# A delta-rule attention and two MoE layers on one core: chunk 1 in half steps, its solve placed first, the merge of one chunk a step later, and weight conversions out of VectorE's written order

## The chip, the cores and the metric

The kernel runs on one core of a Trainium2 chip. The metric is the time of one execution in device microseconds, as the median of three runs. All times below are in microseconds unless they are marked ns.

## The reference, cut to what matters

```python
# attention (4 batches, 8 heads, 768 tokens, head size 48), token by token
k_n = k / (norm(k) + 1e-6)
for t in range(S):
    y[t] = q[t] @ state
    state = state + beta[t] * outer(k_n[t], v[t] - k_n[t] @ state)
# x is y as 3072 tokens by 384 features
h = relu(x @ w_in)                 # 384 -> 2048
x = (h * h) @ w_out                # 2048 -> 384
h = max(x @ w1, x @ w2, x @ w3)    # 384 -> 768, three times
out = h @ w_out2                   # 768 -> 384
```

Everything is float32.

## The kernel before

**The chunks.** The 768 tokens are cut into 12 chunks of 64. Within a chunk the recurrence is a triangular system. Its inverse is computed on VectorE for two chunks at a time: one *solve* covers chunks 0 and 1, the next chunks 2 and 3, and so on. A solve (`solve32`, `solve`) works on M, a tile of 128 rows by 32x32 in the memory `buf`. It has a preparation (`prep`: the norms, ten small instructions, then L239), 30 pairs of a multiply (L285) and an add (L287), and a scaling by a (L288). `finish32` then stores the result to DRAM (`xt`, L325, on SP's queue), and `load_x` loads it again on GpSimd's queue into `xb` (L343) and `x1` (L351). What a solve needs is made by `kkps`: for each of four parts, key products on TensorE (`pk` and `pq`, L182), a copy of `pk` on ScalarE (L199), a masked copy of `pq` on VectorE (L200), and stores to DRAM. `start32` loads M from those stores (L304). The keys of a part come through SP's queue (L169).

**Attention of one chunk** (`attention(c)`) has the steps `st0` (products `pA` and `pY` with the state; VectorE scales v by the norms, L437, and subtracts `pA`, L450), `zz` (`pZ`, needs `xb`), `ww` (`pW`), `mm_u` (`pU`), `st2` (`pY` and the new state), `st3` (transposes, which give `xh` and `xl`, the two float32r parts of the chunk's tokens).

**The first MoE layer** of chunk c (`moe_a(c)`) runs beside attention of chunk c+1. It has 8 `s1` groups of 18 matmuls (`p`, L572), each followed by relu, square and cast on ScalarE (L576 to L578, which gives `gh`) and a subtraction on VectorE (L579, which gives `gl`), and 8 `s2` groups of 12 matmuls (`px`, L590), two `s1` behind. Two `p` tiles exist, so `s1` number n+2 cannot start before `gl` number n is computed. The second MoE layer (L951, L968) follows after the last chunk.

PSUM has two buffers under the tag `at`. `pk`, `pq`, `pA`, `pZ`, `pW`, `pU` and the transposes take them in turn, and the next user waits until the last has been read.

**What sets the order.** `moe_a` is a generator that yields after each `s1` and each `s2`. `steps` runs it and, at chosen steps, advances the other generators: `attention`, `kkps`, a solve, the weight conversions. A list such as `[3, 7, 11]` names the steps. From chunk 1 on, `pin` chains every instruction of TensorE and of VectorE behind the one before it in the written order, so that the scheduler can't move them. ScalarE, GpSimd and SP are ordered by the scheduler. Every engine works through its own order from front to back.

In chunks 9 to 11 the weights of the second MoE layer are loaded and split (`w3load`, `turn`): each piece takes a ScalarE instruction (L103), three on VectorE (L106, L109, L110), a cast on ScalarE (L111) and a subtraction on VectorE (L114). In the written order the four VectorE instructions of a piece stand together.

Of the kernel before, what the change touches and what calls it, by code (L numbers as in the profile page):

```python
# [32 lines left out]
LAG = 2  # L33
# [6 lines left out]
def delta_moe(ctx, tc, kc, ab, kt, vt, beta, beta32, beta16, kq, w_in, w_out, w1, w2, w3, w_out2, out):  # L40
# [32 lines left out]

    after, abs_after, cast_after, raw_after, x_after, raws = [], [], [], [], [], []
    parted, last_gl, last_gh = [], [None], [None]
    NR, NP = 3, NF - 7

    def raw_tile(shape):
# [21 lines left out]
    def turn(raw, hi, lo, shape, lo_eng):  # L100
        t = conv.tile([128, *shape], I32, name="cvt", tag="cvt")
        h, l = raw[..., 1], raw[..., 0]
        g = act.activation(out=t.bitcast(F32), in_=h.bitcast(F32), func=AF.Abs, scale=REBIAS)  # L103
        for i in abs_after:
            behind(g.ins, i)
        g = vec.tensor_scalar(out=t, in0=t, scalar1=3, scalar2=None, op0=ALU.logical_shift_left)  # L106
        for i in after:
            behind(g.ins, i)
        vec.scalar_tensor_tensor(out=h, in0=h, scalar=-0x80000000, in1=t, op0=ALU.bitwise_and, op1=ALU.bitwise_or)  # L109
        vec.scalar_tensor_tensor(out=l, in0=l, scalar=29, in1=h, op0=ALU.logical_shift_right, op1=ALU.bitwise_or)  # L110
        g = act.copy(hi, l.bitcast(F32))  # L111
        for i in cast_after:
            behind(g.ins, i)
        parted.append(lo_eng.tensor_tensor(out=lo, in0=l.bitcast(F32), in1=hi.bitcast(F32), op=ALU.subtract).ins)  # L114

    def signed(raw, t, ahead):
        h, u = raw[..., 1], raw.bitcast(U16)
# [140 lines left out]
    def pin():  # L258
        todo = []
        for i in reversed(nc.cur_bb.bb.instructions):  # L260
            if i.name == seen[0]:
                break
            todo.append(i)
        for i in reversed(todo):
            seen[0] = i.name
            if i.engine in pinned:
                if pinned[i.engine]:
                    behind(i, pinned[i.engine])
                pinned[i.engine] = i
# [113 lines left out]
    def attention(c):  # L383
# [68 lines left out]
        def mm_u(p):  # L452
            x, r = tiles[c, p][2], tiles[c, p][6]
            pU = ps_at.tile([128, U2, D], F32, name="pU", tag="at")
            n = U2 - (0 if not c else 2 if p else 4)
            if c:
                free = pYs[p] if p else pxs
                over = free[0].rearrange("p (b n) -> p b n", b=1) if p else free[0]
                over = over[:, :, DM:DM + 2 * D].rearrange("p b (u d) -> p b u d", d=D)
            order = [u for i in range(U2) for u in (i, n + i) if (i < n if u == i else u < U2)]  # L460
            for u in order:
                for t in range(2):
                    if u < n:
                        pe.matmul(pU[half(t), u], x[half(t), u], r[half(t), u], start=True, stop=True)  # L464
                    else:
                        o = over[half(1 - t), (u - n) // 2, (u - n) % 2]
                        i = pe.matmul(o, x[half(t), u], r[half(t), u], start=False, stop=True, skip_group_check=True)
                        for j in free[1:]:
                            behind(i.ins, j)
            u_ = fresh("u", p, 7, [128, U2, D])  # L470
            on_vec = p and c != 1
            def put(to, po):
                if on_vec:
                    last_vec[0] = vec.tensor_copy(to, po).ins
                else:
                    last_act[0] = act.copy(to, po).ins  # L476
            put(u_[:, 0:n], pU[:, 0:n])
            if c:
                for m in range(n, U2, 2):
                    for t in range(2):  # L480
                        put(u_[half(t), m:m + 2], over[half(1 - t), (m - n) // 2])
# [75 lines left out]
            yield  # L557


    def moe_a(c, gp):  # L560
        px = ps_x2.tile([128, 2, 512], F32, name="px", tag="px")
        pxs[:] = [px]
        gs = {}

        def s1(fp):
            p1 = ps_s1.tile([128, 2, TB], F32, name="p1", tag="p1")
            for j in range(2):
                f = slice(128 * (2 * fp + j), 128 * (2 * fp + j + 1))
                n = 0
                for k in range(KD):  # L570
                    for w, x in ((win_h, xh), (win_l, xh), (win_h, xl)):
                        pe.matmul(p1[:, j], w[:, k, f], x[c][:, k], start=n == 0 and j == 0, stop=n == 8, skip_group_check=True)  # L572
                        n += 1
            gh = gp.tile([128, 2, TB], F32R, name="gh", tag="gh", bufs=LAG + 1)
            gl = gp.tile([128, 2, TB], F32R, name="gl", tag="gl", bufs=LAG + 1)
            act.activation(out=p1, in_=p1, func=AF.Relu)  # L576
            act.activation(out=p1, in_=p1, func=AF.Square)  # L577
            last_gh[0] = act.copy(gh, p1).ins  # L578
            last_gl[0] = vec.tensor_sub(out=gl, in0=p1, in1=gh.bitcast(F32)).ins  # L579
            gs[fp] = (gh, gl)  # L580

        def s2(fp):
            gh, gl = gs.pop(fp)
            for h in range(2):
                hs = slice(128 * h, 128 * (h + 1))
                for j in range(2):
                    f = 2 * fp + j
                    wh_, wl_ = (wout[f // 4][:, i, f % 4] for i in range(2))
                    for i, (x, w) in enumerate(((gh, wh_), (gh, wl_), (gl, wh_))):
                        g = pe.matmul(px[:, h, 0:DM], x[:, j, hs], w, start=f == 0 and i == 0, stop=f == NF - 1 and i == 2, skip_group_check=True)  # L590
                        if f == 0 and i == 0:
                            pxs.append(g.ins)

        for fp in range(NF // 2):
            s1(fp)
            if fp == 1 and sums:
                store_sums()
            yield
            if fp >= LAG:
                s2(fp - LAG)  # L600
                yield
        for fp in range(NF // 2 - LAG, NF // 2):
            s2(fp)
            if fp < NF // 2 - 1:
                yield
        xs = conv.tile([128, 2, DM], F32, name="xs", tag="raw", bufs=NR)
        for h in range(2):
            i = vec.transpose(out=xs[:, h], in_=px[:, h, 0:DM])
            if last_vec[0]:
                behind(i.ins, last_vec[0])  # L610
        sums.append((c, xs))
        if c == NC - 1:
            store_sums()
        yield
# [8 lines left out]
    def steps(main, *others):  # L623

        due = [0.0] * len(others)
        for n, _ in enumerate(main, 1):
            pin()
            for i, (rate, g, *_) in enumerate(others):
                due[i] += rate.count(n) if isinstance(rate, list) else rate
                while due[i] >= 1.0:  # L630
                    due[i] -= 1.0
                    next(g, None)
                    pin()
        for rate, g, *keep in others:
            for _ in () if keep else g:
                pin()
# [64 lines left out]
    if True:  # L701
# [19 lines left out]
        def solve32(g, load=(nc.sync, nc.sync), store=((nc.sync,) * 2,) * 2, landing=0):  # L721
# [9 lines left out]
            for n, i in enumerate(solve(vec, M, 32, 64 * len(HALVED[g]), a, tmp32)):  # L731
                for j in solve_after:
                    behind(i.ins, j)
                ops.append(i.ins)
                if g and n == (24 if g > 1 else 12):
                    norm(nm)
                yield
            finish32(g, M, store)
# [156 lines left out]
        for c in range(NC):  # L895
# [3 lines left out]
                extra += [(1.0, weights(3, 2)), (11 / 15.0, later(3, attention(1))), (4.0, later(20, part(solve_next, 10)))]  # L899
            elif c == 1:  # L900
                pinned.update({first_matmul.ins.engine: None, last_gl[0].engine: None})
                extra += [(4.0, solve_next), ([3, 7, 11, 12, 13, 14, 15], attention(2)), ([4, 5, 6, 7, 8, 9, 9, 10], kkps(HALVED[2], (at,)))]
                solve_after[:] = last_vec
                prep_after.clear()
            elif c + 1 < NC:
                extra.append(([1, 2, 5, 7, 10, 12, 14] if c % 2 else [1, 2, 4, 6, 8, 11, 13], attention(c + 1)))
            if c == 2:
                kc_after.clear()
                solve_after.clear()
                extra.append(([1, 5] + [6 + n * 10 // 32 for n in range(32)], solve32(2, landing=1)))  # L910
            elif c in ahead_:
                extra.append(([1 + n * 14 // 32 for n in range(32)], ahead_[c]))
            if c > 1 and c in KK:
                extra.append(([3, 4, 4, 5, 6, 7, 8, 9], kkps(HALVED[KK[c]], (at,))))
                ahead_[c + 1] = solve32(KK[c], landing=1)
# [6 lines left out]
            if c == NC - 1:  # L922
# [2 lines left out]
                first = []  # L925
                extra.append((0.6, chain(load_w3s, w3load((2,)))))
                extra.append((0.5, later(2, x2_steps(0, wb, first))))
            steps(moe_a(c, gp), *extra)
        after.clear()
        abs_after.clear()  # L930

# [111 lines left out]
```

## Time and profile before

| | |
|---|---|
| median of 3 runs (lowest, highest) | 968.87 (968.15, 968.98) |
| the profiled execution's own time | 970.42 |
| its span, first to last instruction | 968.3 |
| TensorE busy | 879.9 (91%), 11422 matmuls |
| VectorE busy | 502.0 (52%) |
| ScalarE busy | 390.8 (40%) |
| GpSimd busy | 149.8 (15%) |
| mean granted TensorE clock | 0.949 of full speed |

The profiled execution took 1.55 longer than the median. TensorE is busy nine tenths of the span, so what a chunk takes is read from where TensorE waits. The chunks in the span, by TensorE's first `p` matmul of each: chunk 1 from 139.6, chunk 2 from 207.3, chunk 3 from 260.5, chunk 4 from 309.15, chunk 9 from 536.65, chunk 10 from 581.98, chunk 11 from 626.95; the second layer starts at 664.1.

### The profile page before, as it was taken

The numbers are of one execution on the slowest core, as the hardware profiler recorded it, in microseconds if no ns is written. First come the engines' busy times: TensorE is split into PE (matmuls) and PEld (weight loads), VectorE is DVE, ScalarE is ACT, GpSimd is POOL, SyncE is SP. The second block draws the span as 40 slices with busy tenths as digits, with TensorE's granted clock in tenths as the row PEclk, the third lists the DMA queues.
The fourth block names the chain that finished last, engine by engine and source line by source line (L and its number), as shares of the span: only waits on it lengthen the run. The fifth ranks groups of instructions, "written<-read, shape, count | busy, mean of one in ns | idle before, by whom it ended". The sixth has DMA issues, their size and how long they took to land.

```text
span 968.3 us, 26547 instructions
## 1 busy us (share of the span) xinstructions
PE 879.9 (91%) x11422; PEld 851.5 (88%) x11422; DVE 502.0 (52%) x1118; ACT 390.8 (40%) x809; POOL 149.8 (15%) x245
## 2 busy tenths in 40 slices
PE   4449867899699999999999998999999999999998
PEld 4438766889689999999999998998999999999998
DVE  2987957237635862685277446566623323323221
ACT  1666862344244444453445355574412212222211
POOL 2251110322212132212311330001100000000000
PEclk8558988899799999999999999999999999999999
DMA  8987723742274248425632633143300110000000
GB/s 196 320 226 194 216 63 84 191 121 63 52 200 115 71 119 212 109 71 136 150 94 62 146 108 84 51 123 107 112 28 25 37 38 25 26 25 17 17 17 33
DMA packets 121125, 98.83 MB, mean 102 GB/s; under 512 B 75904, under 2 KB 101296, under 8 KB 121008
## 3 DMA queue, kind: packets, MB, share of 16 engines
q1 hardware_dynamic: 100224, 58.23, 23.6%
q0 software_dynamic: 11712, 32.41, 12.4%
q10 hardware_dynamic: 9072, 6.49, 2.3%
q8 instruction: 90, 1.47, 0.7%
q14 instruction: 27, 0.22, 0.1%
HBM read 72.45 MB, written 24.64 MB: 100 GB/s over the span
## 4 chain that ended last, share of the span: by engine, by line
PE 74%; DVE 13%; ACT 6%; DMA 4%; issue 2%; POOL 1%; SPq 0%; ACTq 0%; DVEq 0%; POOLq 0%
PE p L951 23%; PE p L572 17%; PE px L590 17%; PE po L968 8%; DVE buf L285 3%; DVE buf L287 2%; DMA xb<-xt 2%; DVE gl L579 2%; PE pU L464 1%; PE pY L514 1%; ACT p L576 1%; ACT p L577 1%; ACT gh L578 1%; PE pk L182 1%; PE pZ L412 1%
## 5 line engine op out<-in xcount | busy, mean ns | idle before, releaser
L951 PE MATMUL p<-x_h,w 128*128 128x384 f32 x864 | 220.1, 336 | 0.0
L590 PE MATMUL px<-wout,gh 128*128 128x384 f32 x768 | 205.2, 348 | 3.9 <-ACT u L476 1.9
L572 PE MATMUL p<-xh,win_h 128*128 128x256 f32 x576 | 169.6, 294 | 4.1 <-DVE gl L579 2.6
L572 PE MATMUL p<-xl,win_h 128*128 128x256 f32 x576 | 163.8, 285 | 1.5 <-DVE xl L536 1.5
L572 PE MATMUL p<-xh,win_l 128*128 128x256 f32 x576 | 163.9, 285 | 0.0
L951 PEld LDWEIGHTS p<-x_h,w 128*128 128x128 f32 x864 | 156.3, 188 | 0.0
L579 DVE TENSOR_TENSOR gl<-p,gh 128x512 fp32r<-128x512 f32 x96 | 66.2, 690 | 163.4 <-ACT gh L578 158.9
L951 PE MATMUL p<-x_l,w 128*128 128x384 f32 x432 | 145.2, 336 | 0.0
L590 PEld LDWEIGHTS px<-wout,gh 128*128 128x128 f32 x768 | 138.9, 194 | 5.8 <-ACT u L476 2.3
L590 PE MATMUL px<-wout,gl 128*128 128x384 f32 x384 | 131.7, 343 | 2.1 <-DVE gl L579 2.1
L576 ACT ACTIVATE p<-p 128x512 f32<-128x512 f32 x96 | 55.9, 582 | 189.2 <-PE p L572 189.2
L572 PEld LDWEIGHTS p<-xh,win_h 128*128 128x128 f32 x576 | 111.1, 193 | 7.7 <-DVE gl L579 3.1
L572 PEld LDWEIGHTS p<-xl,win_h 128*128 128x128 f32 x576 | 110.8, 193 | 2.0 <-DVE xl L536 1.9
L572 PEld LDWEIGHTS p<-xh,win_l 128*128 128x128 f32 x576 | 111.3, 193 | 0.0
L957 DVE TENSOR_TENSOR mx<-p,mx 128x384 f32<-128x384 f32 x48 | 26.7, 557 | 123.1 <-PE p L951 123.0
L951 PEld LDWEIGHTS p<-x_l,w 128*128 128x128 f32 x432 | 81.2, 188 | 0.0
L590 PEld LDWEIGHTS px<-wout,gl 128*128 128x128 f32 x384 | 74.2, 193 | 2.4 <-DVE gl L579 2.4
L959 ACT CAST hh<-mx 128x384 fp32r<-128x384 f32 x48 | 24.6, 513 | 120.0 <-DVE mx L958 120.0
L287 DVE TENSOR_TENSOR buf<-buf 128x30 f32<-128x30 f32 (+9 forms) x180 | 60.4, 336 | 6.0
L285 DVE TENSOR_TENSOR buf<-buf 128x30 f32<-128x30 f32 (+9 forms) x180 | 60.0, 333 | 5.0
L578 ACT CAST gh<-p 128x512 fp32r<-128x512 f32 x96 | 56.4, 587 | 2.5
L577 ACT ACTIVATE p<-p 128x512 f32<-128x512 f32 x96 | 56.0, 583 | 2.5
(183 smaller groups left out, 1347.9 us busy)
## 6 DMA issues: line engine op xcount, KB each, us to landing
kq<-in_kc_dram POOLq DMA_DIRECT2D x22, 448.0 KB, 5.4
raw<-in_moe_w_dram SPq DMA_DIRECT2D x18, 384.0 KB, 3.2
p<-p POOLq DMA_DIRECT2D x22, 256.0 KB, 3.7
raw<-in_moe_w_out_dram SPq DMA_DIRECT2D x13, 384.0 KB, 3.9
v<-in_vt_dram POOLq DMA_DIRECT2D x24, 192.0 KB, 3.2
ktp<-in_kt_dram POOLq DMA_DIRECT2D x24, 192.0 KB, 3.6
x<-xs SPq DMA_DIRECT2D x48, 96.0 KB, 2.8
xr<-x SPq DMA_DIRECT2D x96, 48.0 KB, 1.9
```

The source lines that it names most:

```text
L285: eng.tensor_tensor(out=tv, in0=M[:, 0:j, j].unsqueeze(2).broadcast_to([u, j, m]), in1=M[:, j, j + 1:n].unsqueeze(1).broadcast_to([u, j, m ...
L287: yield eng.tensor_tensor(out=M[:, 0:j, j + 1:n], in0=M[:, 0:j, j + 1:n], in1=tv, op=ALU.add)
L572: pe.matmul(p1[:, j], w[:, k, f], x[c][:, k], start=n == 0 and j == 0, stop=n == 8, skip_group_check=True)
L576: act.activation(out=p1, in_=p1, func=AF.Relu)
L577: act.activation(out=p1, in_=p1, func=AF.Square)
L578: last_gh[0] = act.copy(gh, p1).ins
L579: last_gl[0] = vec.tensor_sub(out=gl, in0=p1, in1=gh.bitcast(F32)).ins
L590: g = pe.matmul(px[:, h, 0:DM], x[:, j, hs], w, start=f == 0 and i == 0, stop=f == NF - 1 and i == 2, skip_group_check=True)
L951: pe.matmul(p, w[i][:, k, fs], x[:, k], start=n == 0, stop=n == 8)
L957: vec.tensor_max(out=t, in0=ps[1], in1=t)
L959: act.copy(hh[:, f], t2)
L968: pe.matmul(po[:, 0:DM], x[:, f, js], w[:, f], start=i == 0, stop=i == 17)
```

## The change

1. Chunk 1 is run in half steps: `moe_a` yields inside each `s1` and `s2` as well, so there are 32 steps in place of 16, and `steps` has a step 0 ahead of them.
2. In chunk 1, the rest of the solve for chunks 2 and 3 goes into half steps 0 to 13, ahead of attention of chunk 2 (half steps 14 to 31) and of the key products for chunks 4 and 5 (half steps 13 to 23).
3. The solve for chunks 4 and 5 starts in chunk 1: M is loaded at half step 26, and the preparation stands at step 1 of chunk 2 in place of step 5.
4. In `mm_u` of chunk 2, the first half too puts what doesn't fit `pU` into its own `pY` bank and not into `px`.
5. In chunk 9, `zz` and `ww` (the merge) come one step later.
6. The VectorE instructions of `turn` are not chained in the written order.

```diff
+    loose = set()
 ...
-        vec.scalar_tensor_tensor(out=h, in0=h, scalar=-0x80000000, in1=t, op0=ALU.bitwise_and, op1=ALU.bitwise_or)
+        loose.add(g.ins.name)
+        g = vec.scalar_tensor_tensor(out=h, in0=h, scalar=-0x80000000, in1=t, op0=ALU.bitwise_and, op1=ALU.bitwise_or)
+        loose.add(g.ins.name)
 ...
-            if i.engine in pinned:
+            if i.engine in pinned and i.name not in loose:
 ...
-            n = U2 - (0 if not c else 2 if p else 4)
+            own = p or c == 2
+            n = U2 - (0 if not c else 2 if own else 4)
 ...
+                if halves and not j:
+                    yield
 ...
-        for n, _ in enumerate(main, 1):
+        for n, _ in enumerate(chain((None,), main)):
 ...
-                if g and n == (24 if g > 1 else 12):
+                if g and n == 24:
                     norm(nm)
 ...
-                extra += [(4.0, solve_next), ([3, 7, 11, 12, 13, 14, 15], attention(2)), ([4, 5, 6, 7, 8, 9, 9, 10], kkps(HALVED[2], (at,)))]
+                first_solve = [0] * 3 + [1 + n * 13 // 20 for n in range(20)]
+                extra += [(first_solve, solve_next), ([14, 16, 24, 25, 27, 29, 31], attention(2))]
+                ahead_[2] = solve32(2, landing=1)
+                extra += [([13, 14, 18, 19, 20, 21, 22, 23], kkps(HALVED[2], (at,))), ([26], ahead_[2], True)]
 ...
-                extra.append(([1, 2, 5, 7, 10, 12, 14] if c % 2 else [1, 2, 4, 6, 8, 11, 13], attention(c + 1)))
+                extra.append(([1, 2, 5 + c // 9, 7 + c // 9, 10, 12, 14] if c % 2 else [1, 2, 4, 6, 8, 11, 13], attention(c + 1)))
 ...
-                extra.append(([1, 5] + [6 + n * 10 // 32 for n in range(32)], solve32(2, landing=1)))
-            elif c in ahead_:
-                extra.append(([1 + n * 14 // 32 for n in range(32)], ahead_[c]))
+            if c in ahead_:
+                extra.append(([1] * (c == 2) + [1 + (c == 2) + n * (14 - (c == 2)) // 32 for n in range(32)], ahead_[c]))
 ...
-            steps(moe_a(c, gp), *extra)
+            steps(moe_a(c, gp, c == 1), *extra)
```

What moves, at three places. Line numbers of the changed kernel differ: its L290, L292 and L293 are L285, L287 and L288 of before, L205 is L200, L442 and L455 are L437 and L450, L587 is L579, L254 is L249.

**First place, VectorE in chunk 1.** Before, v of chunk 2 is worked on in the middle of the solve (the pairs that work on `buf`):

```order
L285 TENSOR_TENSOR buf<-buf 128x210
L287 TENSOR_TENSOR buf<-buf 128x21x10
L437 TENSOR_TENSOR v<-v,normT 128x384
L450 TENSOR_TENSOR v<-v,pA 128x384
L437 TENSOR_TENSOR v<-v,normT 128x384
L450 TENSOR_TENSOR v<-v,pA 128x384
L285 TENSOR_TENSOR buf<-buf 128x198
L287 TENSOR_TENSOR buf<-buf 128x22x9
```

In the changed kernel the same instructions stand behind the solve's last (L293) and behind the masked copy of the first key product:

```order
L292 TENSOR_TENSOR buf<-buf 128x30
L293 TENSOR_TENSOR buf<-buf,a_1197 128x1024
L205 TENSOR_TENSOR buf<-pq,mask 128x512
L587 TENSOR_TENSOR gl<-p_1964,gh 128x512
L442 TENSOR_TENSOR v<-v,normT 128x384
L455 TENSOR_TENSOR v<-v,pA 128x384
L442 TENSOR_TENSOR v<-v,normT 128x384
L455 TENSOR_TENSOR v<-v,pA 128x384
L587 TENSOR_TENSOR gl<-p_2133,gh 128x512
L205 TENSOR_TENSOR big<-pq,mask 128x512
```

Of the 42 multiplies and adds of the solve that stand in chunk 1, none now waits behind v, and only one of the four masked copies is written near the solve. On TensorE the order of chunk 1 was s1 s1 s1 st0 s2 kk s1 s2 kk s1 s2 kk s1 kk s2 s1 pZ s2 pW s1 pU s2 st2 s2 pT s2, with kk for a part's key products; it is now s1 s1 s1 s2 s1 s2, half s1, kk, half s1, st0 s2 s1 kk s2 kk s1 kk s2 pZ, half s1, pW, half s1, half s2, pU, one s2 long, st2, one s2 long, pT, half s2.

**Second place, VectorE at the start of chunk 2.** Before, the preparation of the next solve (from the copy into ss on) stood behind four `gl`, v of chunk 3 and its transpose:

```order
L608 STREAM_TRANSPOSE xs<-px 128x384 x2
L579 TENSOR_TENSOR gl<-p_2615,gh 128x512
L579 TENSOR_TENSOR gl<-p_2662,gh 128x512
L437 TENSOR_TENSOR v<-v,normT 128x384
L450 TENSOR_TENSOR v<-v,pA 128x384
L437 TENSOR_TENSOR v<-v,normT 128x384
L450 TENSOR_TENSOR v<-v,pA 128x384
L579 TENSOR_TENSOR gl<-p_2763,gh 128x512
L405 STREAM_TRANSPOSE xT<-x_2643 128x256
L579 TENSOR_TENSOR gl<-p_2836,gh 128x512
L249 COPY ss<-buf 128x32
```

Now it stands behind the first `gl`, and v follows it:

```order
L244 TENSOR_TENSOR buf<-buf,r 128x1024
L245 MEMSET buf 128x32
L587 TENSOR_TENSOR gl<-p_2678,gh 128x512
L442 TENSOR_TENSOR v<-v,normT 128x384
L455 TENSOR_TENSOR v<-v,pA 128x384
L442 TENSOR_TENSOR v<-v,normT 128x384
L455 TENSOR_TENSOR v<-v,pA 128x384
L290 TENSOR_TENSOR buf<-buf 128x30
```

The preparation has moved ahead of the second `gl` and of v, by some twenty rows. TensorE's order in chunk 2 is now that of chunk 4 before.

**Third place, chunk 9.** On TensorE `pZ` stood ahead of an `s2` group (`px`):

```order
L572 MATMUL p_7949<-xh,win_l 128x256
L572 MATMUL p_7949<-xl,win_h 128x256
L412 MATMUL pZ<-xb,k_7799 32x32 x32
L590 MATMUL px<-wout_981,gh 128x384 x2
L590 MATMUL px<-wout_981,gl 128x384
```

Now it stands behind that group:

```order
L598 MATMUL px<-wout_981,gh 128x384 x2
L598 MATMUL px<-wout_981,gl 128x384
L417 MATMUL pZ<-xb,k_7797 32x32 x32
L578 MATMUL p_8020<-xh,win_h 128x256
L578 MATMUL p_8020<-xh,win_l 128x256
```

On VectorE, at the end of chunk 9, a whole piece of weights stood between the last `gl` of the chunk and `xl`:

```order
L579 TENSOR_TENSOR gl<-p_8327,gh 128x512
L106 TENSOR_SCALAR cvt<-cvt 128x384
L109 SCALAR_TENSOR_TENSOR raw<-raw,cvt 128x384
L110 SCALAR_TENSOR_TENSOR raw<-raw 128x384
L114 TENSOR_TENSOR w_0_8121<-raw,w_0_8121 128x3x128
L536 TENSOR_TENSOR xl<-pT,xh 128x3x128 x2
```

Now two pieces are under way at once, and the two `xl` stand between their parts (L107, L111, L113 and L118 are L106, L109, L110 and L114 of before):

```order
L587 TENSOR_TENSOR gl<-p_8325,gh 128x512
L107 TENSOR_SCALAR cvt<-cvt 128x384 x2
L111 SCALAR_TENSOR_TENSOR raw<-raw,cvt 128x384
L542 TENSOR_TENSOR xl<-pT,xh 128x3x128
L111 SCALAR_TENSOR_TENSOR raw<-raw,cvt 128x384
L542 TENSOR_TENSOR xl<-pT,xh 128x3x128
L113 SCALAR_TENSOR_TENSOR raw<-raw 128x384
```

The subtraction L114, which needs ScalarE's cast, no longer stands ahead of `xl`.

## Rows read from the trace of the kernel before

**Rows 1.** Stretches, chunks 1 to 4: length, busy PE, PEld, DVE, ACT, POOL; PEclk; DMA.

```profile
139.60:207.30 67.70, 55.19 (x953) 51.50 (x954) 31.00 (x73) 21.78 (x48) 15.54 (x26) 0.87 0.49 128
207.30:260.50 53.20, 44.76 (x697) 42.72 (x697) 38.05 (x99) 19.92 (x45) 6.95 (x11) 0.90 0.23 60
260.50:309.15 48.65, 48.02 (x952) 45.42 (x951) 18.62 (x37) 21.39 (x45) 16.86 (x27) 1.00 0.70 172
309.15:352.54 43.39, 42.31 (x698) 40.98 (x697) 35.19 (x93) 19.73 (x44) 5.74 (x10) 1.00 0.24 66
```

**Rows 2.** Waits of TensorE in chunk 1: total, times, longest.

```profile
PE pk L182 <- DVE v L450: 5.7, 1, 5.7
PE pZ L412 <- DMA xb<-xt: 3.1, 2, 2.2
```

**Rows 3.** Chain of waits in chunk 1: start, duration, what.

```profile
169.92 1.24 DVE buf L288
171.17 1.95 DMA xt<-buf
...
184.50 1.07 PE pZ L412 x62
```

**Rows 4.** VectorE's groups from 145.5 to 171.2: count, busy, mean ns, idle before.

```profile
L287 DVE TENSOR_TENSOR buf<-buf 128x210 f32<-128x210 f32 (+14 forms) x21 | 7.4, 351 | 0.7
L285 DVE TENSOR_TENSOR buf<-buf 128x210 f32<-128x210 f32 (+14 forms) x21 | 7.3, 349 | 0.6
```

**Rows 5.** VectorE in order of time, chunk 1 and start of chunk 2.

```profile
139.80 0.54 DVE L536 TENSOR_TENSOR xl<-pT,xh 128x384 fp32r<-128x384 f32 x1
144.94 0.69 DVE L579 TENSOR_TENSOR gl<-p,gh 128x512 fp32r<-128x512 f32 x1 [4.61 <-ACT gh L578]
...
223.57 0.18 DVE L249 COPY ss<-buf 128x32 f32<-128x32 f32 x1
...
228.84 0.15 DVE L285 TENSOR_TENSOR buf<-buf 128x30 f32<-128x30 f32 x1
```

**Rows 6.** L182 alone, three of the four key products: length, busy PE and PEld.

```profile
166.50:177.00 10.50, 3.48 (x192) 3.07 (x192) 1.00 0.67 171
```

**Rows 7.** Chain of waits in chunks 9 and 10, in order of time.

```profile
543.69 7.45 DMA xb<-xt
...
551.94 3.50 PE px L590 x12
...
560.90 2.15 PE p L572 x18
563.05 2.09 PE px L590 x12
...
577.78 3.16 DMA raw<-in_moe_w_dram
...
613.76 2.00 PE pY L514 x64
```

**Rows 8.** Busy time by stretch: two after a wait, two in chunk 9.

```profile
158.00:162.00 4.00, 3.26 (x68) 2.96 (x69) 3.65 (x12) 0.58 (x1) 0.00 (x0) 0.50 0.00 0
546.00:550.00 4.00, 3.71 (x28) 3.50 (x26) 0.69 (x1) 1.52 (x4) 0.00 (x0) 1.00 1.14 199
550.00:554.00 4.00, 3.01 (x73) 2.91 (x74) 1.04 (x2) 1.77 (x4) 0.00 (x0) 0.83 0.70 177
658.00:662.00 4.00, 1.98 (x12) 1.66 (x10) 3.33 (x7) 0.74 (x2) 0.00 (x0) 1.00 0.01 2
```

**Rows 9.** Waits of TensorE from 490 to 670.

```profile
PE px L590 <- DVE gl L579: 2.1, 1, 2.1
PE p L572 <- DVE gl L579: 1.7, 2, 1.2
PE p L572 <- DVE xl L536: 1.2, 1, 1.2
```

**Rows 10.** DMA issues: KB each, median from issue to landing.

```profile
big<-in_kc_dram SPq DMA_DIRECT2D x9, 448.0 KB, 5.4
```

More of the change, by code (lines that the diff above doesn't have):

```diff
@@ L108, in turn @@
             behind(g.ins, i)
-        vec.scalar_tensor_tensor(out=h, in0=h, scalar=-0x80000000, in1=t, op0=ALU.bitwise_and, op1=ALU.bitwise_or)
-        vec.scalar_tensor_tensor(out=l, in0=l, scalar=29, in1=h, op0=ALU.logical_shift_right, op1=ALU.bitwise_or)
+        loose.add(g.ins.name)
+        g = vec.scalar_tensor_tensor(out=h, in0=h, scalar=-0x80000000, in1=t, op0=ALU.bitwise_and, op1=ALU.bitwise_or)
+        loose.add(g.ins.name)
+        g = vec.scalar_tensor_tensor(out=l, in0=l, scalar=29, in1=h, op0=ALU.logical_shift_right, op1=ALU.bitwise_or)
+        loose.add(g.ins.name)
         g = act.copy(hi, l.bitcast(F32))
@@ L114, in turn @@
         parted.append(lo_eng.tensor_tensor(out=lo, in0=l.bitcast(F32), in1=hi.bitcast(F32), op=ALU.subtract).ins)
+        loose.add(parted[-1].name)
     def signed(raw, t, ahead):
@@ L454, in mm_u @@
             pU = ps_at.tile([128, U2, D], F32, name="pU", tag="at")
-            n = U2 - (0 if not c else 2 if p else 4)
+            own = p or c == 2
+            n = U2 - (0 if not c else 2 if own else 4)
             if c:
-                free = pYs[p] if p else pxs
-                over = free[0].rearrange("p (b n) -> p b n", b=1) if p else free[0]
+                free = pYs[p] if own else pxs
+                over = free[0].rearrange("p (b n) -> p b n", b=1) if own else free[0]
                 over = over[:, :, DM:DM + 2 * D].rearrange("p b (u d) -> p b u d", d=D)
@@ L557, in attention, with moe_a @@
             yield
-    def moe_a(c, gp):
+    def moe_a(c, gp, halves=False):
         px = ps_x2.tile([128, 2, 512], F32, name="px", tag="px")
@@ L592, in s2 @@
                             pxs.append(g.ins)
+                if halves and not h:
+                    yield
         for fp in range(NF // 2):
-            s1(fp)
+            yield from s1(fp)
             if fp == 1 and sums:
@@ L599, in moe_a @@
             if fp >= LAG:
-                s2(fp - LAG)
+                yield from s2(fp - LAG)
                 yield
         for fp in range(NF // 2 - LAG, NF // 2):
-            s2(fp)
+            yield from s2(fp)
             if fp < NF // 2 - 1:
@@ L625, in steps @@
         due = [0.0] * len(others)
-        for n, _ in enumerate(main, 1):
+        for n, _ in enumerate(chain((None,), main)):
             pin()
             for i, (rate, g, *_) in enumerate(others):
-                due[i] += rate.count(n) if isinstance(rate, list) else rate
+                due[i] += rate.count(n) if isinstance(rate, list) else rate * (n > 0)
                 while due[i] >= 1.0:
```

## The prediction

> **What bounds the kernel now.** I read the page first: TensorE is busy nine tenths of the span, so time can only come from where it waits or runs slowly. The second view is the busy time by stretch, one stretch for each chunk [rows 1]. Chunks 1 and 3 do the same on TensorE (953 and 952 matmuls in the records), as do chunks 2 and 4 (697 and 698). Yet chunk 1 takes 67.70 where chunk 3 takes 48.65, and chunk 2 takes 53.20 where chunk 4 takes 43.39. The granted clock is 0.87 and 0.90 in the slow ones and 1.00 in the others. So 19.05 and 9.81 are lost there, 28.9 together.
>
> The waits of TensorE say where in chunk 1 [rows 2]. It waited 5.7 for v: the key products need the `at` buffer that holds `pA`, and v's subtraction stood on VectorE behind some 24 instructions of the solve. It waited again for `xb`, and the chain of waits shows why [rows 3]: the solve's last instruction starts at 169.92, its result is stored from 171.17, and `pZ` starts at 184.50, 13.3 after the store began. After each wait TensorE ran at half its clock for a while: 0.50 from 158 to 162 [rows 8].
>
> In chunks 9 to 11 the views show a second, smaller loss. `xb` lands 7.45 after its issue [rows 7], TensorE is busy 6.72 of 8 around it, and the next `s2` group takes 3.50 where one at full clock takes 2.09 [rows 7, 8]. Three kinds of waits for `gl` and `xl` add 5.0 [rows 9], behind weight pieces on VectorE.
>
> **Chunk 1.** No arithmetic is added; the question is where each queue now stands.
>
> VectorE first. Of the solve 42 instructions are left in chunk 1: 14.7 busy and 1.3 between them, 16.0 in all [rows 4]; one (0.4) now runs before the chunk. VectorE is free from 140.3, where `xl` ends [rows 5]. Four `gl` stand in between, at 0.6 each from one to the next instruction (estimate from 0.69 [rows 5]), and the first waits about 0.3 for ScalarE. So the solve's last starts at 140.3 + 15.6 + 2.4 + 0.3 = 158.6 where it was 169.92, and ends at 159.8. The masked copy of the first key product follows and ends near 160.5.
>
> TensorE next, at 2.15 for an `s1`, 2.09 for an `s2` [rows 7] and 3.48 / 3 = 1.16 for a key product [rows 6]. The first `gl` ended at 145.6 [rows 5]; four ScalarE copies that preceded it now come later, so I take 145.1. From there come `s1`, `s2`, `s1`, `s2`, half an `s1`, a key product and the other half: 11.8, until 156.9. `st0` has as many products as `st2`, which takes 2.00 [rows 7]. Its first half is done at 157.9; its second needs the buffer that the masked copy frees at 160.5. **A wait of 2.6 takes the place of the waits of 5.7, 3.1 and others.** Behind it on TensorE stand all later groups, so it is paid in full.
>
> From 160.5 come half of `st0`, three `s2`, two `s1` and three key products: 1.0 + 6.3 + 4.3 + 3.5 = 15.1, so `pZ` is due at 175.6. `xb` lands at 159.8 + 13.3 = 173.1, in time by 2.5. The keys of the fourth product are a third matter: their load stands in SP's queue behind the second product's use of the same memory, and takes 5.4 [rows 10]; between the two products TensorE has 2.09 + 1.16 + 2.15 = 5.4 of work. I count 0.3.
>
> What the wait of 2.6 does to the clock is not shown. Bounds: nothing, as around 658 to 662, where TensorE stood still for half of 4.00 and the clock stayed at 1.00 [rows 8]; or 3.3, half of the roughly 6.5 at half clock that followed the wait of 5.7. In chunk 9 a wait of 1.3 cost an `s2` group 1.4. I take 2.4, near the upper rows.
>
> So chunk 1 = 48.65 of chunk 3 + 2.6 + 2.4 + 0.3 = 53.9, **13.8 less**. Bounds: 48.65 (19 less), and 60 if a wait for `xb` returns with its clock.
>
> The split of `pU` in chunk 2's attention lies beside matmuls: ScalarE, whose copies TensorE awaited, has two fewer. I count nothing.
>
> **Chunk 2.** Its order on TensorE is chunk 4's, so 43.39 is the base. What differs is the preparation, 5.3 of VectorE (223.57 to 228.84 [rows 5]), which chunk 4 has behind it when it begins. Here it stands ahead of the second `gl` and of v. The first `gl` ended 4.7 after the start of chunk 2 (VectorE's order of time; the row is left out for room); with the preparation, the second `gl` (0.6) and v of the first half (1.1), the `at` buffer is free at 11.7. `pZ` is due at two `s1`, `st0`, `s1`, `s2`: 10.5. That is a wait of 1.2, and I add 0.4 for a later one at the transposes: 45.0, **8.2 less**. Bounds: 43.39, and 53.20 if VectorE holds TensorE as before. M is stored and loaded on the way, with some 5 to spare by the times of before; chunk 3 should stay at 48.65.
>
> **The merge of chunk 9.** One `s2` (2.09) now lies between `pZ` and what it followed. The wait was 8.00 - 6.72 = 1.28 [rows 8], so it is covered, and the slow clock after it goes: 1.4 on that `s2` and 0.3 on the next `s1`. **3.0 less**; bounds 0 and 3.0.
>
> **Conversions.** VectorE waited for ScalarE's casts, with `xl` or `gl` behind them in its order. At the end of chunk 9 two short instructions and one of 0.6 now stand ahead of the first `xl`, and no cast; at the end of chunk 11 eight instructions stand in place of nine, and again no cast. Of the 5.0 of waits [rows 9] I take **4.0**. Bounds: 5.0, and 3.2 lost, one landing of a raw piece [rows 7], since pieces pulled forward can put `xl` behind a load.
>
> **The sum.** 13.8 + 8.2 + 3.0 + 4.0 = 29.0. The profiled execution took 970.42 and would take 941.4; its excess of 1.55 over the median should stay, so from 968.87 I forecast **939.9**.
>
> **The rivals.**
>
> *The wait moves to the loads of chunk 1.* For it: the fourth product's keys have no slack, and the load for chunk 3's attention (448 KB too) and `xb` are under way at once. Against: `xb` has 2.5 to spare. If both land as late as `xb` did in chunk 9 (7.45 [rows 7] in place of 5.4), some 4 are waited and 2 lost to the clock: 946. The Trainium skill (DMA: Bandwidth & Descriptors, Issuing engines are not separate DMA queues) says that transfers issued by SP and by GpSimd end up on the same 16 DMA engines and interleave. By that rule this case is the likelier one, and the trace of chunk 9, with a DMA share of 1.14 [rows 8], agrees.
>
> *The conversions give nothing.* ScalarE's casts still stand in an order that nobody wrote by hand; if the waits only change places: 968.87 - 22 to 25, 945.
>
> *Chunk 2 remains VectorE's.* With 38 of busy time in 45 [rows 1], each `gl` can be late: 948.
>
> *Nothing comes of it*: what the chunks save is given back, since something later is set by loads. Against: chunk 4, which has the same loads behind it, keeps TensorE busy for 42.31 of 43.39 [rows 1]: 968.
>
> *Slower.* M for chunks 4 and 5 comes late at chunk 2's start. Then the copy into ss blocks VectorE, with `gl`, v and the whole solve behind it, and TensorE with them. The stores of the fourth product and M's load must take some 34 longer than I count before it outweighs 29; then 970 and more. Every such landing in the rows is below 8.
>
> **Chances.** Forecast 0.64; loads 0.14; conversions 0.11; chunk 2 0.06; nothing 0.02; slower 0.03. So faster 0.95, same 0.02, slower 0.03, with 0.2% (1.9) as what a measurement of this kernel can tell from no change. The first case alone spans 935 (no clock loss, chunk 2 at its base) to 944. The range for 8 in 10 reaches to the loads, the conversions and chunk 2: 934.5 to 949.
>
> **What would show it.** Right: the solve's last instruction of chunk 1 near 158.6; a wait of TensorE of 2 to 3 for the masked copy (L200) in `st0`; `pZ` near 176 to 178 without a wait for `xb`; chunk 1 at 53 to 55 and chunk 2 at 44 to 46 long; no wait at `pZ` of chunk 9; the waits for `xl` and `gl` at the ends of chunks 9 and 11 below 1. Wrong: a wait for `xb` or for keys in chunk 1, half clock beyond 7 at a stretch, or chunk 3 longer than 49.

## The result and the profile after

The changed kernel takes 944.7 (median of 4 runs, 941.91 to 945.67) where the kernel before takes 968.51 beside it: a ratio of 0.9749, interval 0.9727 to 0.9772, 24 less. Two further comparisons gave 0.9750 (0.9724 to 0.9775) and 0.9769 (0.9748 to 0.9790).

The forecast of 939.9 is 4.8 too low. It lies 0.7 outside the 935 to 944 that the forecast's own case was given, and well inside the range of 934.5 to 949. The first view after is the busy time by stretch, chunks 1 to 4, with the columns of [rows 1].

```profile
142.25:196.66 54.41, 50.32 (x952) 47.35 (x952) 30.04 (x72) 21.79 (x46) 15.60 (x26) 0.97 0.61 152
196.66:244.25 47.59, 44.19 (x697) 42.58 (x697) 37.09 (x100) 19.78 (x45) 6.98 (x11) 0.96 0.25 68
244.25:292.65 48.40, 48.03 (x951) 45.42 (x951) 18.46 (x37) 21.41 (x45) 16.90 (x27) 1.00 0.74 179
292.65:336.01 43.36, 42.28 (x697) 40.95 (x697) 35.34 (x93) 19.74 (x44) 5.75 (x10) 1.00 0.25 66
```

Chunks 3 and 4 are what they were; chunk 1 lost 13 and chunk 2 lost 5.6. The same cut through all chunks, from the first matmul of `p` in one to that in the next (TensorE's order of time; the second layer to the start of TensorE's last matmul), for three profiles of the changed kernel:

| stretch | before | forecast | after, three profiles |
|---|---|---|---|
| chunk 0 | 62.9 | as before | 65.5, 63.6, 63.2 |
| chunk 1 | 67.5 | 53.9 | 54.4, 55.2, 58.4 |
| chunk 2 | 53.2 | 45.0 | 47.6, 46.1, 46.1 |
| chunks 3 to 8 | 276.3 | as before | 274.4, 275.5, 275.6 |
| chunks 9 to 11 | 127.3 | 120.3 | 119.0, 119.0, 119.1 |
| second layer | 300.6 | as before | 300.6, 300.6, 300.8 |

The waits of TensorE in chunks 1 and 2 after (columns of [rows 2]):

```profile
PE pt L282 <- DVE Sb L505: 2.5, 1, 2.5
PE pA L451 <- DVE buf L205: 1.7, 1, 1.7
PE pW L426 <- issue: 1.7, 1, 1.7
PE pZ L417 <- DVE v L455: 0.9, 1, 0.9
```

The waits of 5.7 for v and 3.1 for `xb` in [rows 2] are gone. The wait for the masked copy (L205) was forecast, as was that for v at chunk 2's `pZ`. At chunk 2's transposes (`pt`) 0.4 was forecast on top of chunk 4, which has a wait of 1.1 there itself; the 2.5 is 1.4 more. The fourth was not forecast: the profile puts it down to "issue", which means that it shows nothing that TensorE waited for. The chain of waits in chunk 1 has the forecast wait and the unforeseen one (start, duration, what; compare [rows 3]; the "issue" in the first row is the solve's last instruction at work, from 160.98):

```profile
161.02 1.11 issue
162.13 0.70 DVE buf L205
...
164.68 3.15 PE px L598 x12
...
182.15 0.63 PE pW L426 x47
182.78 1.66 issue
184.44 0.26 PE pW L426 x6
```

In chunks 9 to 11 the waits of [rows 9] have shrunk to the second of these (TensorE, 470 to 645; the first, 1.1 at `pt`, was there before too), and where `xb` held TensorE in [rows 8] it is busy throughout:

```profile
PE pt L282 <- DVE Sb L505: 1.1, 1, 1.1
PE p L578 <- DVE gl L587: 0.5, 1, 0.5
```

```profile
528.00:532.00 4.00, 4.00 (x31) 4.00 (x30) 0.69 (x1) 1.52 (x4) 0.00 (x0) 1.00 1.04 216
532.00:536.00 4.00, 4.00 (x88) 3.71 (x87) 1.04 (x2) 1.89 (x4) 1.06 (x2) 1.00 0.65 158
```

### The profile page after: what moved, and what is told of

It reads as the page before. It is cut to its first block, busy times and chain, and to the rows that moved or that the text cites. A ratio compares the mean times of both kernels' runs of the same rounds, so it can differ in the third digit from the quotient of the medians.

```text
span 942.3 us, 26555 instructions
## 1 busy us (share of the span) xinstructions
PE 875.7 (93%) x11422; PEld 848.9 (90%) x11422; DVE 498.9 (53%) x1118; ACT 391.6 (42%) x807; POOL 150.9 (16%) x245
## 4 chain that ended last, share of the span: by engine, by line
PE 81%; DVE 7%; ACT 6%; DMA 4%; issue 2%; ACTq 0%; SPq 0%; DVEq 0%
PE p L963 24%; PE px L598 20%; PE p L578 19%; PE po L980 8%; DMA rawp<-in_moe_w_in_dram 2%; PE pU L470 2%; PE pY L520 1%; DVE gl L587 1%; PE pk L187 1%; DVE buf L290 1%; PE pA L451 1%; DVE buf L292 1%; DMA raw<-in_moe_w_out_dram 1%; PE pW L426 1%; PE pZ L417 1%
## 5 line engine op out<-in xcount | busy, mean ns | idle before, releaser
L587 DVE TENSOR_TENSOR gl<-p,gh 128x512 fp32r<-128x512 f32 x96 | 66.3, 690 | 154.5 <-ACT gh L586 154.3
L292 DVE TENSOR_TENSOR buf<-buf 128x30 f32<-128x30 f32 (+9 forms) x180 | 60.5, 336 | 6.0
L290 DVE TENSOR_TENSOR buf<-buf 128x30 f32<-128x30 f32 (+9 forms) x180 | 59.9, 333 | 4.8
```

The source lines that it names most:

```text
L290: eng.tensor_tensor(out=tv, in0=M[:, 0:j, j].unsqueeze(2).broadcast_to([u, j, m]), in1=M[:, j, j + 1:n].unsqueeze(1).broadcast_to([u, j, m ...
L292: yield eng.tensor_tensor(out=M[:, 0:j, j + 1:n], in0=M[:, 0:j, j + 1:n], in1=tv, op=ALU.add)
```

## The experiments

The edits are to the changed kernel unless said otherwise; ratios are to the kernel before. No run puts chunk 1's old order back alone: what its new order gave is read from its own waits, before and after. Since chunk 0 and chunk 1 vary by 2 to 4 from execution to execution (the last run below), a part's size is read from its own chunk in the profile, and the time only confirms the sign.

**Conversions pinned again** (`e1_pinned`).

```
-            if i.engine in pinned and i.name not in loose:
+            if i.engine in pinned:
```

> The changed kernel, with the weight conversions held in the written order again. By the prediction's step (waits of 5.0 for gl and xl in chunks 9 to 11, of which 4.0 were to go) it takes 4.0 more: chunks 9 to 11 together 4 longer than the 119.0 of the changed kernel, the other chunks as they are, 948.7. Rival (a): the free conversions also shortened chunks 3 to 8, which are 1.9 shorter than before; then those come back too and it takes 5 to 7 more, 950 to 952. Rival (b): the free conversions are what made chunk 0 longer (65.50 where it was 62.85); then 2.6 of the loss is given back, and chunk 0 is near 62.9 here.

Measured 949.14, ratio 0.9794 (0.9775 to 0.9812). Chunks 9 to 11, in the busy time by stretch:

```profile
517.62:559.85 42.23, 42.23 (x695) 40.82 (x695) 17.94 (x35) 22.54 (x48) 15.65 (x26) 1.00 0.59 145
559.85:604.22 44.37, 42.55 (x632) 41.02 (x631) 27.28 (x56) 25.28 (x54) 0.00 (x0) 1.00 0.27 73
604.22:641.40 37.18, 34.44 (x241) 33.91 (x241) 23.15 (x44) 21.88 (x41) 0.00 (x0) 1.00 0.38 108
```

They sum to 123.8, 4.8 more than with free conversions: the prediction's step, slightly larger. Chunks 3 to 8 take 276.7, the top of a spread that reaches from 274.4 to 276.4 with free conversions, so rival (a) is not shown. Chunk 0 is 63.1, but rival (b) falls below.

**Merge at its old steps** (`e2_merge`).

```
-([1, 2, 5 + c // 9, 7 + c // 9, 10, 12, 14] if c % 2 ...
+([1, 2, 5, 7, 10, 12, 14] if c % 2 ...
```

> The changed kernel with the merge of chunk 9 at its old steps (5 and 7). By the prediction's step 3.0 more, 947.7: chunk 9 at 45.2 where it is 42.21, with a wait for xb at pZ and a clock below 1.00 behind it. Rival: the free conversions alone keep the wait away, since what stood ahead of the transfer's issue was late for their sake; then chunk 9 stays within 0.5 of 42.2 and the time within 1 of 944.7.

Measured 947.19, ratio 0.978 (0.9754 to 0.9807), which cannot tell 0 from 3. The chunk can: 42.73, not 45.2, at full clock.

```profile
520.12:562.85 42.73, 42.50 (x696) 41.18 (x696) 20.28 (x43) 23.39 (x49) 15.58 (x26) 1.00 0.58 143
```

With free conversions the later merge is worth 0.5 in this profile, and the rival holds here; the next run, which has the merge at its old steps too, shows that it does not always hold. With pinned conversions the merge is worth 3.1 (45.33 before, 42.23 in the run above).

**The conversions alone on the kernel before** (`e7_loose`; the edit is the diff's `loose` lines).

> The kernel before with nothing changed but the conversions, which are free in VectorE's order. By the prediction's sum it gains 4.0, all in chunks 9 to 11, and the chunk 9 wait for xb (1.28, and 1.75 of clock) stays: 964.9. By the second run's reading (with the merge at its old steps chunk 9 lost only 0.5) chunk 9 gains 2.6 from the conversions too, chunks 3 to 8 some 2, chunks 10 and 11 some 5: 9 less, 959 to 960, and 962 if chunk 0 is at 65.4 in place of 62.8.

Measured 964.39, ratio 0.9947 (0.9928 to 0.9966), some 5 less. Chunks 9 to 11 take 120.4, which is 6.9 less: 1.8, 2.8 and 2.4. The rest of the second reading fails, since chunks 3 to 8 gain only 1.6 and chunk 2 is 1.0 longer. What is left in chunk 9 (43.56) stands in the waits of TensorE as

```profile
PE pZ L417 <- issue: 0.9, 1, 0.9
PE pZ L417 <- DMA xb<-xt: 0.2, 1, 0.2
```

The profile names nothing for the 0.9, but this too is a wait for `xb`. Its first half lands at 548.28 and `pZ` starts at 548.37. The same 0.09 lies between the two in the kernel before (550.76 and 550.85) and in `e2_merge` (533.20 and 533.29), and behind each of these the second half is waited for (before: landed at 551.14 by [rows 7]). So the wait for `xb` is 1.1 here, hardly less than the 1.3 of before, and most of the 1.8 that chunk 9 gains is clock: the granted clock stays at 1.00 from 547 to 555 here, where it fell to 0.83 before [rows 8]. Whether the conversions keep it up is not shown.

**Second solve begun in chunk 2** (`e3_solve`).

```
-([26], ahead_[2], True)
-[1] * (c == 2) + [1 + (c == 2) + n * (14 - (c == 2)) // 32 ...
+[1, 5] + [6 + n * 10 // 32 ...]      (for chunk 2)
```

> The changed kernel with the solve for chunks 4 and 5 begun in chunk 2, as before. By the prediction's step the early start was worth 8.2; measured, chunk 2 became 5.6 shorter (53.18 to 47.59). So chunk 2 goes back to 53 and the time to 950.3, if the early start alone shortened it. Rival: part of the 5.6 came from chunk 1, whose late work no longer runs into chunk 2, or from the sums placed elsewhere (own); then chunk 2 stays at 49 to 51, and the time at 946 to 948.

Measured 952.3, ratio 0.9824 (0.9804 to 0.9844). Chunk 2 is back at 53.57, its clock at 0.90, with a wait of 6.0 at the transposes, as before. All of chunk 2's gain is the early start's. The time is 2.0 more than expected; chunk 1 is 57.0 here, within its spread.

```profile
199.09:252.66 53.57, 45.01 (x696) 42.76 (x696) 38.29 (x100) 19.92 (x45) 6.95 (x11) 0.90 0.23 61
```

**First key product three half steps earlier** (`e4_key`).

```
-([13, 14, 18, 19, 20, 21, 22, 23], kkps(HALVED[2], (at,)))
+([10, 11, 18, 19, 20, 21, 22, 23], kkps(HALVED[2], (at,)))
```

> The changed kernel with the first key product of chunk 1 three half steps earlier, so that its masked copy stands among the solve's instructions on VectorE and not behind the last. The prediction's step says that this copy is what the second half of st0 waits for (1.68 measured, and the clock at 0.64 in the 4 behind it): then the wait goes, and 3 to 3.5 with it: chunk 1 at 51, 941.5. The solve's last ends 0.6 later. Rival: TensorE is held by the solve anyway (v, then xb), and the wait comes back some groups later at pA's buffer or at pZ; then chunk 1 stays at 54 to 55, 944 to 945.

Measured 947.65, ratio 0.9778 (0.9756 to 0.98). The masked copy's wait is gone, as expected, and chunk 1 is 56.8, no shorter. Its waits of TensorE, and a stretch behind them (columns of [rows 1]):

```profile
PE pW L426 <- issue: 1.9, 1, 1.9
PE pZ L417 <- DMA xb<-xt: 1.8, 2, 1.6
```

```profile
179.25:183.25 4.00, 2.10 (x27) 1.90 (x16) 0.00 (x0) 1.45 (x4) 1.00 (x2) 0.50 0.97 338
```

TensorE now reaches `pZ` ahead of `xb`, and the clock is at 0.50 behind it. The rival holds in kind: the wait comes back at `pZ`, and the time is longer than the rival said. Two things moved. TensorE is ready for `pZ` 34.6 after the chunk's start, where it was 37.9 in the changed kernel; and the two parts of `xb` land at 36.0 and 36.5, where they landed at 33.4 and 33.7. So in the changed kernel `xb` had 4.1 to spare, where I had counted 2.5, but its landing is not fixed.

**Preparation of chunk 2 at the end of chunk 1** (`e5_prep`, and again as `e5_again`).

```
-([26], ahead_[2], True)
+([26, 31], ahead_[2], True)
-[1] * (c == 2) + [1 + (c == 2) + n * (14 - (c == 2)) // 32 for n in range(32)]
+[1 + n * 14 // 32 for n in range(32)]
```

The second edit also starts the solve's steps in chunk 2 one step earlier, as chunk 4 has them.

> The changed kernel with the preparation of the solve for chunks 4 and 5 moved from behind the first gl of chunk 2 to the last half step of chunk 1, where VectorE waits 3.15 for that gl, and the solve's steps spread from the first step of chunk 2 as in chunk 4. The account of the result: chunk 2 is 4.2 longer than chunk 4 (47.59 and 43.36) because 5.3 of preparation keep VectorE late, until TensorE waits 0.86 at pZ and 2.52 at the transposes, with some 1.4 of half clock behind it. Then both waits go: chunk 2 at 43.4 to 44, 940.5 to 941. Rival: M is not landed when chunk 1 ends, and VectorE, which works in order, holds the first gl of chunk 2 back; then a wait for gl of 1 to 4 stands at the start of chunk 2, and the time is 943 to 946.

> The changed kernel with the preparation of chunk 2 moved to the end of chunk 1, once more and with more rounds. Its chunk 2 was 44.84 where the changed kernel has 46.1 to 47.6, so it takes 1.3 to 2.7 less than the run beside it, 942 to 943. Rival: what it gains in chunk 2 it loses in chunk 1 (57.23 in its first profile, with the clock at 0.59 behind pW); if that belongs to the order and is no chance, the two take the same within 1.

Measured 942.75, ratio 0.9723 (0.9698 to 0.9747), and 943.63, ratio 0.9729 (0.9707 to 0.9752), where the changed kernel beside them took 946.41 and 946.29. Chunk 2 is 44.84 and 44.02. TensorE's waits there in the second profile are those of chunk 4 (1.1 at `pt`); in the first the rival's wait for `gl` adds 1.1.

```profile
PE pt L282 <- DVE Sb L505: 1.1, 1, 1.1
PE p L578 <- DVE gl L587: 0.2, 1, 0.2
```

The preparation fills a gap of VectorE's. In the changed kernel (first row) VectorE waits 3.15 for the first `gl` of chunk 2 before it prepares; in this one (the others) the preparation runs there, and `gl` follows with no wait:

```profile
201.12 0.69 DVE L587 TENSOR_TENSOR gl<-p,gh 128x512 fp32r<-128x512 f32 x1 [3.15 <-ACT gh L586]
```

```profile
199.20 0.18 DVE L254 COPY ss<-buf 128x32 f32<-128x32 f32 x1
...
202.97 1.23 DVE L244 TENSOR_TENSOR buf<-buf,r 128x1024 f32<-128x1024 f32 x1
...
205.21 0.65 DVE L587 TENSOR_TENSOR gl<-p,gh 128x512 fp32r<-128x512 f32 x1
```

By the medians this kernel is 3.7 and 2.7 faster than the changed one beside it; each interval alone overlaps with the changed kernel's, but chunk 2 is 1.3 to 3.6 shorter in every pair of profiles, about 2.5. Chunk 1 is 57.2 and 56.7, inside the changed kernel's 54.4 to 58.4, so a loss there is not shown.

**Both, with pZ and pW half a step later** (`e12_keyprep`: `e5_prep`, the key list of `e4_key`, and attention(2) at 25 and 26 in place of 24 and 25).

> The kernel of the run before, and in chunk 1 the first key product three half steps earlier (no wait for the masked copy), with pZ and pW half a step later, so that xb is less late for them (1.59 when the key product alone was moved). If the waits in chunk 1 add up, it is 53 long and the time 939 to 941. Rival: TensorE stops at the end of its instruction block (1.7 to 2.7) and its clock falls behind whichever wait comes first; then chunk 1 stays at 55 to 57 and the time equals that of the run before.

Measured 942.91, ratio 0.9728 (0.9707 to 0.9749): the same as without. Chunk 1 is 56.5, as the rival said, but mostly for another reason: the stop in `pW` is 0.9, and the waits for `xb`, which lands later here than in `e4_key`, are 4.3.

```profile
PE pZ L417 <- DMA xb<-xt: 4.3, 2, 3.3
PE pW L426 <- issue: 0.9, 1, 0.9
```

**Twenty more matmuls at the start** (`e9_warm`: `NWARM = 28`).

> The changed kernel with 20 more matmuls on zeros at the very start (28 in place of 8), which are 40 more pairs of instructions on TensorE ahead of everything else and change nothing that is computed. In every kernel so far TensorE stops in chunk 1 after 58 of the 64 matmuls of pW, for 0.6 to 2.7, with no releaser shown. If it waits there for its own next instructions, the stop moves with their count: after 18 of the 64, or out of pW by a group. If it waits for data (a part of k or xT), it stays at 58. The time itself is not what is asked; the extra matmuls lie in the wait for the first keys, 13.9, and may cost some us.

One run, 944.83. Chunk 0 is 58.6 and chunk 1 60.3; together they take as long as in other profiles. The 64 matmuls of `pW` run through, and the stop is in another group:

```profile
PE pD L498 <- issue: 2.2, 1, 2.2
```

How many matmuls TensorE had behind it at such a stop is in the busy time from the span's start to it. Of after, `e12_keyprep`, and this run, with the count behind PE's busy time:

```profile
0.00:184.43 184.43, 129.63 (x2251) 120.11 (x2251) 129.00 (x308) 99.22 (x191) 46.31 (x79) 0.78 0.71 186
```

```profile
0.00:185.12 185.12, 126.58 (x2251) 117.38 (x2252) 128.46 (x308) 100.09 (x193) 45.55 (x79) 0.81 0.73 193
```

```profile
0.00:192.77 192.77, 138.69 (x2505) 127.61 (x2506) 130.95 (x313) 104.32 (x205) 51.43 (x89) 0.82 0.71 190
```

The profile's page of the changed kernel says in how many blocks TensorE's instructions come (first row: matmuls and weight loads; second: packets, MB):

```profile
PE 875.7 (93%) x11422; PEld 848.9 (90%) x11422; DVE 498.9 (53%) x1118; ACT 391.6 (42%) x807; POOL 150.9 (16%) x245
...
q8 instruction: 90, 1.47, 0.7%
```

That is 22844 / 90 = 253.8 instructions, or 126.9 matmuls with their loads, in a packet of 16 KB. All such stops of over 0.2 in all profiles stand at 222, 2251, 2505, 3519, 3647, 5296 or 6947 matmuls (within 1), and 222 plus 16, 18, 26, 27, 40 or 53 times 126.9 gives these within 3. (The "issue" at `pZ` of chunk 9, matmul 8342, lies near such an edge too, but `xb` ended it, as said above.) So TensorE stops at the end of its own instruction block, and not for data: the edges stay at their counts when other matmuls are put there. In `e12_keyprep` `pW` starts nine matmuls later; the stop is again at 2251, now after 49 of the 64. Here I had expected the stop at 18 of 64, the old edge moved by 40 pairs; that edge passed without one, and a later edge had it.

**Sums of chunk 2's first half as before** (`e8_own`: `own = p`).

> The changed kernel with the sums of the first half of chunk 2's attention placed as before (own for the second half alone). The prediction counted nothing for this part: then within 1 of the changed kernel. Rival: ScalarE's two further copies in chunk 1 hold u back, which TensorE awaits; then chunk 1 is 0.5 to 1.5 longer, with a wait for u ahead of pY.

Measured 945.96, ratio 0.9756 (0.9734 to 0.9778), beside 0.9769 of the changed kernel: no difference in the time. In chunk 1 the rival's wait is there, 0.7, where the changed kernel has none:

```profile
PE px L598 <- ACT u L482: 0.7, 1, 0.7
```

**The changed kernel again** (`e8_again`, `e8_third`).

> The changed kernel itself, once more, beside the others. Chunk 0 was 65.50 in its profile, 65.3 and 65.4 in two kernels that do the same there, and 62.8 in a third. If the length of chunk 0 belongs to the order of the instructions, it is 65.4 again; if it is a matter of chance from execution to execution, it can be 62.8, and the times of one kernel lie in two groups some 2.6 apart. The other chunks within 0.5 of 54.4, 47.6, 48.4, 43.4, but for chunk 1, which I have seen from 54.4 to 55.3.

> The changed kernel itself, beside the next three on one chip. 944 to 946; chunk 0 at 63.6 or 65.4 by chance, chunk 1 at 54.4 to 55.3 where the clock stays up behind pW and 57 where it falls, chunk 2 at 46.1 or, with half clock behind its wait of 2.5, at 47.5.

Measured 946.41 and 946.29. Chunk 0 is 63.6 and 63.2 where the first profile had 65.5, so its length varies with the order unchanged, and rival (b) of the first experiment falls. Chunk 1 is 55.2 and 58.4: in the last, TensorE stopped 2.7 in `pW`, and its clock was at 0.79 for the 8 from 182 on. Chunk 2 shows that the same wait can leave the clock alone. The wait of 2.5 at `pt` in the first profile, and in the second:

```profile
229.50:233.50 4.00, 2.00 (x7) 2.00 (x8) 3.83 (x11) 1.32 (x6) 1.02 (x2) 0.73 0.78 234
233.50:237.50 4.00, 4.00 (x27) 4.00 (x27) 2.86 (x10) 0.00 (x0) 0.00 (x0) 0.84 0.00 0
```

```profile
228.60:232.60 4.00, 2.00 (x12) 2.00 (x13) 3.83 (x11) 1.32 (x6) 1.02 (x2) 1.00 0.73 234
232.60:236.60 4.00, 4.00 (x33) 4.00 (x32) 2.86 (x10) 1.42 (x3) 0.00 (x0) 1.00 0.00 0
```

## Why the prediction was right, and where it was off

- **VectorE's queue in chunk 1: right.** The solve's last instruction was forecast 19.0 after the chunk's start and came at 160.98, 18.7 after it.
- **The wait of 2.6 for the masked copy: right in kind, 0.9 too large.** It is 1.7 in every run that keeps that order. The 2.4 for the clock measures 1.8: the second half of `st0` took 1.7 in place of 1.0, the `s2` behind it 3.15 in place of 2.09.
- **pZ without a wait for xb: right**, 180.1 where I gave 176 to 178, in a chunk that began 2.6 later. The first rival (loads late in chunk 1) did not happen in this kernel, nor did the 0.3 for the keys of the fourth product. It lay close: in `e4_key` and `e12_keyprep`, where TensorE comes earlier and `xb` lands later, it is there.
- **Chunk 1's 13.8: missed a term.** Measured 13.1, 12.3 and 9.1. The missing term is the stop at an instruction block's edge in `pW`, 0.6 to 2.7 with the clock behind it now and then. The sum has nothing for it; before, such stops took 0.3 to 0.6.
- **Chunk 2's 8.2: mis-sized.** Measured 5.6, 7.1 and 7.1. The wait at `pZ` was right (1.2 forecast, 0.9 measured). The "0.4 for a later one at the transposes" is 1.4 (2.5, of which chunk 4, the base, has 1.1), and sometimes some 1.5 of clock. I nearly let VectorE's lateness end at `pZ`, but it has 37 of busy time in 46 there and carries it on; `e5_prep` takes the preparation out, and both waits are back at chunk 4's. The third rival (VectorE's chunk) is a part of the truth.
- **The merge's 3.0 and the conversions' 4.0: right in kind, 7.0 forecast, 8.3 measured.** With the conversions pinned the merge gives 3.1, and freeing them then gives 4.8 (`e1_pinned`), so 0.8 of the miss is the conversions'. The step "the wait was 1.28", put down to `xb`, holds, although the waits of before name "issue" for 1.15 of it. What I did not see is that both edits touch chunk 9: the conversions alone give 6.9, 1.8 of it there, and then the merge adds 0.5 to 1.4 only.
- **The sum: in range, partly by misses that cancel.** In the first profile chunk 0 gave 2.6 too much by chance, chunk 1 0.5 and chunk 2 2.6; chunks 3 to 8 gave 1.9 back (mostly chance: 274.4 is the lowest of the spread), chunks 9 to 11 1.3. That is 2.5 of the 4.8. The rest is the profiled execution's own place: before, it stood 1.55 above the median that I took off again; after, at 944.06, it stands 0.6 below its median. Two rivals named 946 and 945, close to what was measured; neither mechanism is what made the difference (no load was waited for in chunk 1, and the conversions did give their part).

Open: why the clock falls behind some of the waits and not behind others of the same length, and why chunk 0 has several lengths. No run here was made for either.

## What to carry to other kernels

When a queue is cleared at one place, follow its lateness to the end of the stretch, and not to the next wait alone. Two edits that touch the same loss do not add up (in chunk 9, 3.1 and 1.8 alone, 3.1 together); price each with the other already made. Where a profile names nothing for a wait, look at what landed just before it ended, and at whether the count of instructions is the same each time. Before an instruction is moved forward, look for a gap of its engine at the place to which it goes: the preparation moved by half a step into a wait of 3.15 gave about 2.5, while an earlier key product only moved TensorE into the next wait.

## What the hardware showed

TensorE can stop at the edge of an instruction block while the DMA engines are busy: 1.66 with a DMA share of 0.99 in the 4 around it.

```profile
182.00:186.00 4.00, 2.34 (x77) 2.11 (x76) 0.00 (x0) 1.18 (x4) 2.19 (x5) 1.00 0.99 294
```

The packet of the instruction queue (`q8`) tells more. In the first profile it started at 182.27, and TensorE went on at 184.44. In all 45 such stops of over 0.2 in the fourteen profiles the last packet started 2.2 to 2.9 before TensorE went on, however long the stop was. (At matmul 8342, where the wait was for `xb`, it had started 6.9 before.) So the stop ends with the block's arrival. Beyond the first edge, all 32 stops have a DMA share of 0.60 or more in the 4 around the packet's start, and none of the 447 crossings with a share under 0.3 has a stop. That the stop is at the edge is shown; that the busy DMA engines make the block late fits all of these, but no run changed their load alone.

The Trainium skill (Runtime: NRT & Kernel Launch, Instruction fetch mechanics) says that instructions come in blocks of 16 KiB, 256 instructions each, over a queue of the engine's own, and that crossing into the next block is mostly hidden. The trace agrees on the blocks and on "mostly": of the 88 later crossings in a profile, one to three stop for over 0.2. The one in the new chunk 1 cost 0.6 to 2.7 in all twelve profiles that have it.
